# Cosine attention and hard-swish feed-forward on one core: tensors relaid, instruction order fixed by hand, feed-forward matmuls spread over the attention, one activation table

## The chip, the cores and the metric

One core of one Trainium2 chip runs the whole program; the other seven are idle. The metric is device time in microseconds (us) of that core. Each kernel was run several times, beside runs of the kernel before on the same chip; a figure such as 771.4 us is the median of the runs. Profiles are of one execution, so the span on a profile page differs a little from the median.

## The reference, cut to what matters

```python
# q, k, v: (8 batches, 12 heads, 448 tokens, 64) float32; tau = 0.1
q_n = q / (norm(q) + 1e-6);  k_n = k / (norm(k) + 1e-6)      # over the last axis
scores = q_n @ k_n.T / tau
attn = exp(scores - max);  attn = attn / (sum(attn) + 1e-9)
x = (attn @ v), as (3584 tokens, 768)
h = x @ w_in                        # 768 x 2048
g = h * clip(h + 3, 0, 6) / 6       # hard swish
out = g @ w_out                     # 2048 x 768, float32
```

Cosine scores lie between -10 and 10, so neither kernel takes the maximum off before the exponential. Both compute in bf16 with fp32 sums.

## The kernel before

Two heads of a batch are one *pair*; there are 48. Tokens are cut in four chunks of 112. Results of TensorE (PE) go to PSUM, the memory that ScalarE and VectorE then read them from. A *bank* here is a piece of PSUM of 128 x 512 fp32, and a *tile* is a named buffer of one or two banks. A *unit* is the group of matmuls that fills one bank with a part of a feed-forward layer; to *evacuate* it is to read it out, which frees the bank. The parts that the argument touches:

```python
    def attention_pre(b, hp, slot):           # loads and norms
        nc.gpsimd.dma_start(out=qk_t[:CH, 0:8, :], in_=q_r[:, b, hA : hA + 2, :, :])   # casts to bf16
        ...  # k, v likewise; squares and reduce_sum on VectorE
        nc.scalar.activation(out=ln_t[:CH, :], in_=n2_t[:CH, :], func=AF.Ln)
        nc.scalar.activation(out=r_t[:CH, :], in_=ln_t[:CH, :], func=AF.Exp, scale=-0.5)
    ...
    def attention_core(b, hp, emit_backfill):
        for c in range(NCH):
            ...  # sc_ps = scores of 112 keys x 448 queries, both heads
            nc.scalar.activation(out=attn_t[:CH, :, :], in_=sc_ps[:CH, :, :S], func=AF.Exp, scale=inv_tau)
            nc.tensor.matmul(pv_ps[:, 0, :S], v_t[:CH, c, :], attn_t[:CH, 0, :], ...)   # [v, ones] stationary
            ...
            if c == 1:
                emit_backfill(1)
        nc.scalar.activation(out=lnd_t[D:128, :, :], in_=pv_ps[D:128, :, :S], func=AF.Ln)
        nc.scalar.activation(out=recd_t[D:128, :, :], in_=lnd_t[D:128, :, :], func=AF.Exp, scale=-1.0)
        ...  # xT = values * recd_t, on VectorE
    ...
    def moe_mm1_unit(blk, fc, half):          # one unit of the first layer
        ps1 = psum.tile([128, S], FP32, name="mm1_ps", tag="moe", bufs=4)
        ...  # six matmuls; relu on ScalarE or clip on VectorE; product on VectorE
```

The line numbers in the profile: L189 and L196 are scores, L203 the exponential, L209 and L216 values, L228 and L229 the logarithm and the exponential that together make the reciprocal of the softmax sums, L128 and L129 the same for the norms, L263 and L310 the two feed-forward layers. The order on each engine is left to the framework's scheduler.

## Time and profile before

| | kernel before |
|---|---|
| median time | 771.4 us |
| PE, VectorE (DVE), ScalarE (ACT), GpSimd (POOL) busy | 72%, 52%, 71%, 26% |
| table loads on ScalarE | 180, 231.0 us |
| PE waits for an exponential (L203) | 155.1 us (score matmuls 96.4, value matmuls 58.7) |
| first first-layer matmul | 59 us |

A busy share is an average over the span, so it does not say what the bound is; the chain that ended last does, and the waits say who held whom. A group line of the profile reads: source line, engine, operation, output and inputs, shape, how often; then busy us and mean ns of one; then the idle time of the engine just before it and what ended that. A wait line reads: who waited for whom, us in total, how often, the longest. The lines of this kernel are in the prediction below.

### The profile page before, as it was taken

What the parts mean: (1) busy time and instruction counts of PE and PEld (TensorE: products, weight loads), DVE (VectorE), ACT (ScalarE), POOL (GpSimd) and SP (SyncE); (2) the same over time, 40 slices, a digit from 0 to 9 for tenths busy, and PEclk for the clock granted to TensorE, in tenths of its full rate; (3) what the DMA queues carried; (4) which work ended last, traced back from release to release, by engine and by line L of the source; (5) the groups of instructions that cost most, each with busy time, mean ns of one, the idle gap of its engine ahead of it and who ended that gap; (6) DMA issues with size and microseconds to landing.
All of it is one profiled execution on the core that took longest, in us unless ns stands there. A gap on an engine that the chain in (4) does not pass through costs nothing.

```text
span 770.8 us, 7902 instructions
## 1 busy us (share of the span) xinstructions
PE 557.4 (72%) x2816; PEld 291.3 (38%) x2816; DVE 399.1 (52%) x682; ACT 549.6 (71%) x628; POOL 198.2 (26%) x316
## 2 busy tenths in 40 slices
PE   2546648656776767676866676789687799984998
PEld 1223214322333334343433333445344355542464
DVE  5645646666565625333755666334566633452722
ACT  3799897888798897788788889655678752466200
POOL 9435543323323222212223132222122110000000
PEclk9999668877789989999879999989899999998899
DMA  9969975535516334414435225332233012100011
GB/s 72 101 81 124 107 95 36 37 22 38 37 12 43 40 42 52 44 37 44 31 23 33 18 20 45 49 56 63 27 21 22 7 38 76 44 0 1 1 73 71
DMA packets 142600, 34.34 MB, mean 45 GB/s; under 512 B 132576, under 2 KB 141792, under 8 KB 142560
## 3 DMA queue, kind: packets, MB, share of 16 engines
q0 software_dynamic: 134496, 22.82, 38.5%
q1 hardware_dynamic: 8064, 11.01, 3.9%
q8 instruction: 22, 0.36, 0.2%
q14 instruction: 18, 0.15, 0.1%
HBM read 45.61 MB, written 11.01 MB: 73 GB/s over the span
## 4 chain that ended last, share of the span: by engine, by line
ACT 55%; PE 35%; issue 5%; DVE 4%; DMA 1%; POOL 1%; ACTq 0%; DVEq 0%; POOLq 0%
ACT attn_t L203 16%; PE mm_ps L310 12%; PE mm_ps L263 9%; ACT L203 7%; ACT L228 6%; ACT L128 6%; ACT L129 5%; ACT lnd_t L228 5%; PE sc_ps L189 4%; ACT recd_t L229 4%; PE pv_ps L209 4%; PE sc_ps L196 3%; PE pv_ps L216 3%; ACT hs_r L272 2%; ACT L229 2%
## 5 line engine op out<-in xcount | busy, mean ns | idle before, releaser
L203 ACT ACTIVATE attn_t<-sc_ps 112x896 bf16<-112x896 f32 x192 | 175.6, 915 | 140.2 <-PE sc_ps L196 120.2
L263 PE MATMUL mm_ps<-xT,w_in_sb 128*128 128x448 bf16 x768 | 192.6, 388 | 18.6 <-DVE xT L235 7.5
L310 PE MATMUL mm_ps<-w_out_sb,gT 128*128 128x384 bf16 x896 | 167.1, 336 | 4.0 <-DVE o_t L318 4.0
L189 PE MATMUL sc_ps<-qT_sb,bd_ka 128*112 128x448 bf16 x192 | 78.6, 410 | 104.6 <-ACT attn_t L203 96.4
L235 DVE TENSOR_TENSOR xT<-pv_ps,recd_t 64x448 bf16<-64x448 f32 x96 | 59.2, 617 | 149.6 <-ACT recd_t L229 145.6
L209 PE MATMUL pv_ps<-attn_t,v_t 112*128 112x448 bf16 x192 | 78.3, 408 | 61.0 <-ACT attn_t L203 58.7
L263 PEld LDWEIGHTS <-w_in_sb 128*128 128x128 bf16 x768 | 81.0, 106 | 97.3 <-issue 46.0
L310 PEld LDWEIGHTS <-gT 128*128 128x128 bf16 x896 | 89.5, 100 | 67.5 <-issue 11.2
L163 POOL MEMSET bd_ka<- 64x448 bf16 x48 | 22.4, 466 | 269.5 <-PE sc_ps L189 232.3
L196 PE MATMUL sc_ps<-qT_sb,bd_kb 128*112 128x448 bf16 x192 | 79.5, 414 | 0.0
L216 PE MATMUL pv_ps<-attn_t,v_t 112*128 112x448 bf16 x192 | 78.4, 408 | 0.0
L318 DVE TENSOR_SCALAR o_t<-mm_ps 128x384 f32<-128x384 f32 x56 | 30.7, 556 | 85.3 <-PE mm_ps L310 85.0
L196 PEld LDWEIGHTS <-bd_kb 128*112 128x112 bf16 x192 | 28.3, 148 | 122.3 <-issue 116.4
L120 POOL DMA_DIRECT2D qk_t<-in_q_dram x48 | 39.5, 823 | 112.8 <-DVE kn_t L136 112.3
L279 DVE SCALAR_TENSOR_TENSOR gT<-hs_r,mm_ps 128x448 bf16<-128x448 bf16 x64 | 39.6, 619 | 44.0 <-ACT hs_r L272 43.4
L228 ACT ACT_TABLE_LOAD x47 | 60.3, 1283 | 0.8
L127 DVE TENSOR_REDUCE n_t<-sq_t 112x16 bf16<-112x1024 bf16 x48 | 57.9, 1215 | 0.8
L216 PEld LDWEIGHTS <-v_t 112*128 112x128 bf16 x192 | 20.6, 107 | 96.9 <-issue 91.7
L272 ACT ACTIVATE hs_r<-mm_ps,three_bias 128x448 bf16<-128x448 f32 x64 | 40.0, 630 | 23.5 <-PE mm_ps L263 20.7
L128 ACT ACT_TABLE_LOAD x43 | 55.2, 1283 | 1.5 <-PEq L390 0.7
L203 ACT ACT_TABLE_LOAD x42 | 53.9, 1283 | 1.5 <-PE sc_ps L196 0.8
L122 POOL DMA_DIRECT2D v_t<-in_v_dram x48 | 39.4, 820 | 53.3 <-PE pv_ps L216 44.6
(33 smaller groups left out, 623.2 us busy)
## 6 DMA issues: line engine op xcount, KB each, us to landing
out_dram<-o_t SPq DMA_DIRECT2D x56, 192.0 KB, 1.9
qk_t<-in_q_dram POOLq DMA_DIRECT2D x48, 112.0 KB, 3.3
qk_t<-in_k_dram POOLq DMA_DIRECT2D x48, 112.0 KB, 3.7
v_t<-in_v_dram POOLq DMA_DIRECT2D x48, 112.0 KB, 3.3
w_in_sb<-in_moe_w_in_dram POOLq DMA_DIRECT2D x6, 512.0 KB, 7.4
w_out_sb<-in_moe_w_out_dram POOLq DMA_DIRECT2D x16, 192.0 KB, 6.3
```

What stands on the lines that cost most here:

```text
L127: nc.vector.reduce_sum(n2_t[:CH, :], sq_t[:CH, :, :], axis=AX.X)
L128: nc.scalar.activation(out=ln_t[:CH, :], in_=n2_t[:CH, :], func=AF.Ln)
L189: nc.tensor.matmul(sc_ps[:CH, 0, :S], bd_ka[:, c * CH : (c + 1) * CH], qT_sb[:, :], start=True, stop=True,)
L196: nc.tensor.matmul(sc_ps[:CH, 1, :S], bd_kb[:, c * CH : (c + 1) * CH], qT_sb[:, :], start=True, stop=True,)
L203: nc.scalar.activation(out=attn_t[:CH, :, :], in_=sc_ps[:CH, :, :S], func=AF.Exp, scale=inv_tau,)
L209: nc.tensor.matmul(pv_ps[:, 0, :S], v_t[:CH, c, :], attn_t[:CH, 0, :], start=(c == 0), stop=(c == NCH - 1),)
L216: nc.tensor.matmul(pv_ps[:, 1, :S], v_t[:CH, 4 + c, :], attn_t[:CH, 1, :], start=(c == 0), stop=(c == NCH - 1),)
L228: nc.scalar.activation(out=lnd_t[D:128, :, :], in_=pv_ps[D:128, :, :S], func=AF.Ln)
L235: nc.vector.tensor_tensor(out=xT[p0 : p0 + 64, h // 2, b * S : (b + 1) * S], in0=pv_ps[0:D, hh, :S], in1=recd_t[D:128, hh, :], op=ALU.mult,)
L263: nc.tensor.matmul(ps1[:, :], w_in_sb[:, cc, fc * 128 : (fc + 1) * 128], xT[:, cc, tcol : tcol + S], start=(cc == 0), stop=(cc == CC - 1),)
L272: nc.scalar.activation(out=r_hs[:, :], in_=ps1[:, :], func=AF.Relu, bias=three_bias[:, :], scale=1.0,)
L310: nc.tensor.matmul(ps2[:, :], gT[:, fc, tci * 128 : (tci + 1) * 128], w_out_sb[:, fc, m * MH : (m + 1) * MH], start=(fc == 0), stop=(fc == ...
```

## The change

The intent is to make TensorE (PE) the bound and to keep it busy. The kernel is rewritten nearly whole, so only the core of the diff is shown:

```diff
+    ctx.enter_context(tc.manual_schedule())                       # fixed order
+    nc.scalar.preload_act_table_set("natural_log_exp_and_others") # one table
 ...
-    CH = 112
-    NCH = S // CH
+    SM = 384              # three chunks of 128 tokens of each head,
+    SR = S - SM           # and one of the last 64 tokens of both heads
 ...
+    X = [psum.tile([128, 2, 512], FP32, name=f"X{i}", tag=f"X{i}") for i in range(3)]
+    Y = psum.tile([128, 512], FP32, name="Y", tag="Y")
+    Z = psum.tile([128, 1024], BF16, name="Z", tag="Z")
+    moe_banks = [X[2][:, 0, :], X[2][:, 1, :], Y[:, :]]
 ...
-        nc.gpsimd.dma_start(out=qk_t[:CH, 0:8, :], in_=q_r[:, b, hA : hA + 2, :, :])
+            nc.sync.dma_start(out=raw[:, :, 4 * n : 4 * n + 3, :], in_=main(t))   # fp32, runs of 768 bytes
 ...
-            nc.tensor.matmul(pv_ps[:, 0, :S], v_t[:CH, c, :], attn_t[:CH, 0, :], ...)
+                nc.tensor.matmul(o, at[:, n, q_cols(i // HP, j)], mv, ...)        # exp stationary, [v, 1] moving
 ...
-        nc.scalar.activation(out=lnd_t[D:128, :, :], in_=pv_ps[D:128, :, :S], func=AF.Ln)
-        nc.scalar.activation(out=recd_t[D:128, :, :], in_=lnd_t[D:128, :, :], func=AF.Exp, scale=-1.0)
+        nc.vector.reciprocal(out=rc[:, :, :], in_=pv4[:, :, :, D])
 ...
+    for f in range(4):                                            # all weights, after pair 2's squares
+        nc.gpsimd.dma_start(out=w_in_sb[:, :, f * FG : (f + 1) * FG], ...)
+    for f in range(4):
+        nc.gpsimd.dma_start(out=w_out_sb[:, 4 * f : 4 * f + 4, :], ...)
 ...
+    for i in range(NP):                                           # 48 pairs, four slots each
+        for s in range(4):
+            ...                                                   # ns: this slot's share of feed-forward work
+            scores(i, s, next_sc(i))                              # two matmuls, one exp
+            if s == 0:
+                ...
+                fill(0.6 * ns); values(i - 1, 3); finish_values(i - 1); fill(0.4 * ns)
+            ...
+            else:
+                fill(ns)
+                values(i, 2)
```

(The slot loop is put on fewer lines here.) Squares, normalisation and the cast of v go to GpSimd (for the first two pairs, squares and normalisation stay on VectorE). Relus of the first layer are all on ScalarE and products all on VectorE. In the lines of the profile after, L163 are scores, L167 the exponential, L195 values, L238 and L267 the two layers, L248 the relu and L251 the product that read a first-layer unit out of PSUM.

## The prediction

> **What bounds the kernel now.** I read the page first (busy shares and the chain that ended last), then the groups of instructions by line, then the waits, then one pair of heads in order of time. The page, engine shares and the chain by engine:
>
> ```profile
> PE 557.4 (72%) x2816; PEld 291.3 (38%) x2816; DVE 399.1 (52%) x682; ACT 549.6 (71%) x628; POOL 198.2 (26%) x316
> ...
> ACT 55%; PE 35%; issue 5%; DVE 4%; DMA 1%; POOL 1%; ACTq 0%; DVEq 0%; POOLq 0%
> ```
>
> No engine is full, and over half of the chain lies on ScalarE (ACT). The groups by line say what ScalarE does with it:
>
> ```profile
> L203 ACT ACTIVATE attn_t<-sc_ps 112x896 bf16<-112x896 f32 x192 | 175.6, 915 | 140.2 <-PE sc_ps L196 120.2
> ...
> L228 ACT ACT_TABLE_LOAD x47 | 60.3, 1283 | 0.8
> ...
> L128 ACT ACT_TABLE_LOAD x43 | 55.2, 1283 | 1.5 <-PEq L390 0.7
> L203 ACT ACT_TABLE_LOAD x42 | 53.9, 1283 | 1.5 <-PE sc_ps L196 0.8
> ```
>
> With the loads of L129 (43.6 us) and L229 (18.0 us) in the longer list these are 180 loads, 231.0 us: 30% of the span, and 42% of ScalarE's busy time. The waits show the ping-pong that results: the score matmuls, the exponential and DVE's last multiply wait for one another.
>
> ```profile
> DVE xT L235 <- ACT recd_t L229: 145.6, 46, 11.9
> ACT attn_t L203 <- PE sc_ps L196: 120.2, 76, 11.4
> ...
> PE sc_ps L189 <- ACT attn_t L203: 96.4, 58, 6.6
> ```
>
> And the end of one pair, in order of time (start, length):
>
> ```profile
> 486.43 1.28 ACT L228 ACT_TABLE_LOAD   x1
> ...
> 487.73 0.91 ACT L228 ACTIVATE lnd_t<-pv_ps 64x896 f32<-64x896 f32 x1
> ...
> 488.66 1.28 ACT L229 ACT_TABLE_LOAD   x1
> ...
> 489.95 0.95 ACT L229 ACTIVATE recd_t<-lnd_t 64x896 bf16<-64x896 f32 x1
> ...
> 490.93 1.25 DVE L235 TENSOR_TENSOR xT<-pv_ps,recd_t 64x448 bf16<-64x448 f32 x2 [5.84 <-ACT recd_t L229]
> ```
>
> The reader is to see 4.4 us of ScalarE for one reciprocal of softmax sums, more than half of it loads, while PE has only feed-forward work to fill with. Before 59 us there is none, and PE is busy 50.4 of the first 100 us, there mostly with starts 0.37 us apart instead of 0.19.
>
> **What the Trainium skill says.** (1) "ScalarE: Activation LUTs", What ACT_TABLE_LOAD costs: about 1283 ns a load, plus a drain of about 1380 ns; its section on table sets says that one set has both exp and ln. The trace agrees on 1283; no drain shows, the next activation starts some 20 ns after the load. (2) "TensorE: Matmul & The Clock Gate", Back-to-back issue gap: N/2.4 + 2.5 ns, so 189 ns for 448 columns and 162 for 384. Agrees: six L310 matmuls take 1.14 us, that is five gaps of 0.16 and one whole 0.34. For short matmuls with a weight load each the page gives about 81 ns at N=128; the trace differs, since four 112-column transposes start 50 ns apart. (3) "GPSIMD Engine Reference", Elementwise, side by side: 4497 ns for a tensor_tensor over 2048 fp32, some 2.2 ns an element; no run here shows it. (4) "DMA: Bandwidth & Descriptors", Queues, rings and completion order: an engine takes turns between queues, packet by packet. The trace can't show turns; in its first 115 us the DMA row stands near full.
>
> **The change part by part.**
>
> *ScalarE.* One table load is left: minus 230 us. The reciprocal leaves ScalarE (minus 43.8 + 45.4). Remaining: exponentials 144 x 0.915 + 48 of half size (0.915 - 448/1.2 ns = 0.54) = 158; relus 128 x 0.63 = 81 (twice as many as now); norms 96 x 0.213 = 20; half the output copies 28 x about 0.51 = 14. Sum 273 us against 549.6. ScalarE ceases to be the bound.
>
> *DVE.* Per pair: reduction 896/1024 of 1.215 = 1.08; four copies out of the transposes about 1.25; reciprocal and 512-element multiply 0.1 + 0.69; copy back 0.39; two small ones 0.13: 3.65 x 48 = 175. Feed-forward 128 x 0.62 = 79, output copies 28 x 0.56 = 16. Sum 270: under now's 399. GpSimd: square and normalise 896 fp32 elements at 2.2 ns each, plus a 512-element cast of about 0.8: an estimate of 4.8 us a pair from page (3), so 225 us; hidden later, near the pace in the first phase.
>
> *PE.* The built program has 3872 matmuls: 768 x 189 = 145; 896 x 162.5 = 146; scores 336 x 189 = 63.5; transposes 528 x 56 = 29.6; values with exp(scores) stationary and 65 moving columns 1344 at a chosen 45 ns (estimate, below the 50 ns of the 112-column transposes) = 60.5. Sum **444 us**. So PE is now the floor, if nothing makes it wait.
>
> *The start.* The order puts no feed-forward matmul ahead of pair 7, and before that stand 22.8 of the 444 us. Until then pairs run at the latency of the chain score, exp, values, transpose and copies, or at GpSimd's 4.8 us, or PE's 6.5 us at half clock: about 5.5 x 7 after some 16 us of loads and normalisation before the first exp (which stands behind two more pairs' norms in ScalarE's order) = 55. All weights are now asked for at about 10 us, together with the loads. Weights are 12.6 MB of HBM reads; between 57.8 and 77 us, with full queues, the kernel before landed 124 GB/s in bf16, so read about twice that in fp32: some 50 us of all DMA, and each pair's 0.69 MB takes turns with it. I add 10: first feed-forward matmul at **65 us**.
>
> *The new wait.* The order of waits in the built program matters most. Three PSUM banks take turns, but two of them are halves of one tile X2, and I traced each matmul's semaphore value back to its producer: a unit that enters the second half of X2 waits for the DVE read of the unit **just before it**, in the first half, though the data differ. So each third unit starts only after its predecessor is evacuated. The price from the trace: from the start of the last matmul to the activation 0.44 (499.17 to 499.61), relu 0.63, step 0.04, DVE 0.62, step 0.04 = 1.77, less the gap of 0.19: 1.58 us (1.57 in the sums). There are 42 such entries after first-layer units, and attention matmuls between cover 0.08 us of it on average: 62.6 us. 19 after second-layer units, 0.85 us each with 0.32 cover: 13.2. Entries two units behind add 4.7. Sum **80.5 us** of bare PE stall. ScalarE and DVE are each some 45% busy (273 and 270 of 603) with other things, of 0.4 to 1.9 us at a time and in strict order (DVE's norms wait for two activations in the middle): 0.4 us more on each of 61 entries and 0.2 on 43 others = **33**.
>
> *Sum:* 65 + (444 - 22.8) + 80.5 + 33 + 3 for the last store = **603 us**. Gain: 168 us.
>
> **The rivals.** (A) *Dense PE.* If the bank waits cost little, 65 + 421 + 3 + some 10 = about 500. For it: the author spreads work by the nanosecond, and the stretch 600 to 680 us of the kernel before already runs PE 76.3 of 80 us busy. Against: the waits stand in the program, and nothing but 0.08 us stands between. (B) *The exponential becomes the bound again.* In the steady part all scores use one double bank X0, so scores s+1 wait for exp s: 0.44 + 0.915 + 0.04 = 1.4 us, against 1.55 us of fill per slot. Relus ahead of it in ScalarE's order can push it over: 164 slots x 0.3 = 50 us more, so about 650. Partly the same time as the bank stalls, so I don't add it. (C) *A slow start.* If loads are really starved until the weights are in, pair 7 starts at 85 or 90: about 625. The DMA row near full in the kernel before speaks for it; 768-byte runs where there were 256-byte ones (132,576 of 142,600 packets are now under 512 B) speak against. (D) *Short matmuls with their weight loads cost 80 ns*, as page (2) has it: 1344 x 35 = 47 more. Against: the 50 ns transposes.
>
> **Range and chances.** The floor that I can hardly doubt is 45 + 415 + 70 + 3 = 533; B, C and D each add 20 to 50 and seldom all. I take 545 to 660. To come within 2% of now, 755, three of the rivals would have to be full size at once: faster 0.97.
>
> **What would show it.** One ACT_TABLE_LOAD and ScalarE near 270 us. PE busy or pipelined most of the span, the chain over half PE. In the waits: PE on the first-layer line waiting for DVE's gT line, some 40 to 60 times at 1.5 to 2.2 us, sum 80 to 110 us; the same for the second layer, 10 to 25. First first-layer matmul at 55 to 80 us. Value matmuls some 45 ns apart. GpSimd's two-input operations near 2 us. I am wrong if those bank waits are few or short (A), if PE's longest sum is on exp (B), or if the first 100 us hold the time (C).

## The result, and the profile after

The changed kernel takes 627.7 us (625.8 to 629.7) against 771.4 us. The ratio is 0.814 (95% interval 0.811 to 0.817). A ratio is the mean time of one kernel's runs over that of the other's runs of the same rounds, so it isn't quite the ratio of the medians. Executions over 1.5% slower than the fastest of the same kernel are left out of the means. All outputs are right.

The page of the kernel after, engine shares and the chain by engine:

```profile
PE 468.8 (75%) x3872; PEld 282.0 (45%) x3872; DVE 284.5 (46%) x667; ACT 260.4 (42%) x445; POOL 187.9 (30%) x154
...
PE 54%; DVE 18%; ACT 12%; DMA 7%; issue 5%; SPq 3%; POOL 0%; DVEq 0%; ACTq 0%; POOLq 0%
```

ScalarE went from 549.6 to 260.4 us and from 55% to 12% of the chain. PE now leads it, but a quarter of the span PE does nothing. The groups by line that matter, and after them one of PE's waits in front of the scores, to which later runs are compared:

```profile
L238 PE MATMUL X<-xT,w_in_sb 128*128 128x448 bf16 x510 | 122.9, 356 | 78.3 <-DVE gT L251 77.7 <-DVE o L281 0.5
L267 PE MATMUL X<-w_out_sb,gT 128*128 128x384 bf16 x608 | 118.5, 328 | 20.9 <-ACT o L279 9.4 <-DVE gT L251 7.6 <-DVE o L281 3.9
...
L238 PE MATMUL Y<-xT,w_in_sb 128*128 128x448 bf16 x258 | 62.0, 359 | 0.0
...
L54 ACT ACT_TABLE_LOAD x1 | 1.3, 1283 | 0.7 <-PEq L431 0.7
```

```profile
PE X L163 <- ACT at L167: 15.5, 17, 6.4
```

In both feed-forward layers all of the waiting stands in front of matmuls into X (here the tile X2, of two banks). Matmuls of these layers into Y, a tile of one bank, never waited. One such wait, in order of time (start, length; in square brackets the idle time before):

```profile
300.76 1.11 PE L238 MATMUL X<-xT,w_in_sb 128*128 128x448 bf16 x5
...
301.91 0.63 ACT L248 ACTIVATE u<-X,half_bias 128x448 bf16<-128x448 f32 x1
302.57 0.62 DVE L251 SCALAR_TENSOR_TENSOR gT<-u,X 128x448 bf16<-128x448 bf16 x1 [1.13 <-ACT u L248]
...
303.25 0.92 PE L238 MATMUL X<-xT,w_in_sb 128*128 128x448 bf16 x4 [1.26 <-DVE gT L251]
```

A unit ends in one half of X2, its relu and its product run one after the other, and only then does PE write the other half. The beginning, from the chain in order of time (start, length, what):

```profile
18.34 7.94 DMA raw<-in_q_dram
26.30 9.76 DMA raw<-in_q_dram
36.08 13.22 DMA raw<-in_q_dram
49.31 12.51 DMA raw<-in_q_dram
```

From 18 to 62 us the chain is almost nothing but loads. The first feed-forward matmul starts at 79 us, later than in the kernel before. The span cut there (columns as in the busy shares; the count of instructions in brackets; then PE's clock, DMA's share, GB/s):

```profile
0.00:79.00 79.00, 36.77 (x323) 23.20 (x324) 40.93 (x111) 26.88 (x49) 40.36 (x40) 0.83 0.89 185
79.00:624.00 545.00, 432.04 (x3551) 258.79 (x3548) 243.61 (x556) 233.53 (x396) 147.50 (x115) 0.99 0.24 67
```

So two questions are open: what do the bank waits cost, and what holds up the beginning? And a third: which part of the change made the gain?

### The profile page after: what moved, and what is told of

It reads as the page before. It is cut to its first block, busy times and chain, and to the rows that moved or that the text cites. A ratio compares the mean times of both kernels' runs of the same rounds, so it can differ in the third digit from the quotient of the medians.

```text
span 624.0 us, 9913 instructions
## 1 busy us (share of the span) xinstructions
PE 468.8 (75%) x3872; PEld 282.0 (45%) x3872; DVE 284.5 (46%) x667; ACT 260.4 (42%) x445; POOL 187.9 (30%) x154
## 4 chain that ended last, share of the span: by engine, by line
PE 54%; DVE 18%; ACT 12%; DMA 7%; issue 5%; SPq 3%; POOL 0%; DVEq 0%; ACTq 0%; POOLq 0%
PE X L267 15%; PE X L238 13%; DVE gT L251 7%; PE X L163 7%; PE Y L267 7%; DMA raw<-in_q_dram 7%; ACT u L248 6%; PE X L195 6%; DVE n L110 5%; PE Y L238 4%; ACT at L167 3%; DVE xT L222 2%; PE Z L221 1%; PE Z L133 1%; DVE o L281 1%
## 5 line engine op out<-in xcount | busy, mean ns | idle before, releaser
L167 ACT ACTIVATE at<-X 128x896 bf16<-128x896 f32 x192 | 156.6, 820 | 152.4 <-PE X L163 152.2
L238 PE MATMUL X<-xT,w_in_sb 128*128 128x448 bf16 x510 | 122.9, 356 | 78.3 <-DVE gT L251 77.7
L120 POOL TENSOR_TENSOR nrm<-raw,r 128x896 bf16<-128x896 f32 x46 | 77.8, 1691 | 225.6 <-DVE r L114 225.6
L238 PEld LDWEIGHTS <-w_in_sb 128*128 128x128 bf16 x768 | 72.9, 99 | 138.6 <-issue 86.3
L267 PE MATMUL X<-w_out_sb,gT 128*128 128x384 bf16 x608 | 118.5, 328 | 20.9 <-ACT o L279 9.4
L267 PEld LDWEIGHTS <-gT 128*128 128x128 bf16 x896 | 85.2, 98 | 78.6 <-issue 26.8
L163 PE MATMUL X<-qT,kz 128*128 128x448 bf16 x336 | 102.0, 376 | 17.8 <-ACT at L167 15.5
L101 POOL TENSOR_TENSOR sq<-raw 128x896 f32<-128x896 f32 x46 | 77.4, 1684 | 107.1 <-DMA raw<-in_q_dram 61.1
L251 DVE SCALAR_TENSOR_TENSOR gT<-u,X 128x448 bf16<-128x448 bf16 x85 | 52.7, 620 | 97.5 <-ACT u L248 96.5
L195 PE MATMUL X<-vx,at 128*128 128x65 bf16 (+1 forms) x1344 | 75.0, 204 | 19.7 <-ACT at L167 19.7
L195 PEld LDWEIGHTS <-at 128*128 128x128 bf16 x1344 | 66.9, 102 | 48.3 <-ACT at L167 22.1
L248 ACT ACTIVATE u<-X,half_bias 128x448 bf16<-128x448 f32 x85 | 53.6, 631 | 38.8 <-PE X L238 36.9
L238 PE MATMUL Y<-xT,w_in_sb 128*128 128x448 bf16 x258 | 62.0, 359 | 0.0
L110 DVE TENSOR_REDUCE n<-sq 128x14 f32<-128x896 f32 x48 | 51.7, 1077 | 18.9 <-POOL sq L101 18.8
L267 PE MATMUL Y<-w_out_sb,gT 128*128 128x384 bf16 x288 | 56.1, 326 | 0.0
L163 PEld LDWEIGHTS <-kz 128*128 128x128 bf16 x336 | 31.0, 102 | 35.6 <-issue 19.6
L251 DVE SCALAR_TENSOR_TENSOR gT<-u,Y 128x448 bf16<-128x448 bf16 x43 | 26.6, 619 | 16.2 <-ACT u L248 15.6
```

The lines of the kernel that those rows point to most:

```text
L101: eng.tensor_tensor(out=sq[:, :, :], in0=a, in1=a, op=ALU.mult)
L110: nc.vector.tensor_reduce(out=n2[:, :], in_=sq[:, :, :], axis=AX.X, op=ALU.add)
L120: eng.tensor_tensor(out=nrm[:, :, :, :].rearrange("p s h d -> p h s d"), in0=raw_of[i][:, :, :, :], in1=r_of[i][:, :].rearrange("p (h s) - ...
L163: nc.tensor.matmul(sc[:, n, 0:S], k_block(i, name), qT_of[i][:, :], start=True, stop=True)
L167: nc.scalar.activation(out=at[:, 0:m, :], in_=sc[:, 0:m, 0:S], func=AF.Exp, scale=inv_tau)
L195: nc.tensor.matmul(o, at[:, n, q_cols(i // HP, j)], mv, start=(name == "A0" and j % 2 == 0), stop=last, skip_group_check=True,)
```

## The experiments

Theory: (1) units wait for each other because two of the three banks belong to one tile (the *false wait*: the data differ), and this costs about 110 us; (2) the beginning is long because all weights are moved beside the first loads; (3) the table loads were most of the old bound. Each has a rival in the expectations.

### e1_rotation: another order of the banks

```diff
-        return moe_banks[bank_n[0] % 3]
+        return moe_banks[(0, 2, 1, 2)[bank_n[0] % 4]]
```

> Only the order in which feed-forward units take the three banks is changed: first half of X2, Y, second half of X2, Y. No unit then waits for the one just before it; 124 wait for the one two before. Theory (the shared tile makes the stalls): first-layer PE waits on gT fall from 77.7 us to 25 to 45, second-layer ones from 20.9 to under 8; time 628 -> 565 to 590. Rival (ScalarE and VectorE in their fixed order are the pace, the bank only shows it): the wait moves to scores on exp or to other banks, time above 610.

Measured: 547.1 us, ratio to before 0.709 (0.707 to 0.711): 80.6 us less than the changed kernel, and 18 us under the range that I had written, since the false wait costs more than the 98.6 us of listed waits by which I had reckoned (see e2). The waits that stay:

```profile
PE Y L238 <- DVE gT L251: 19.2, 25, 2.6
...
PE X L238 <- DVE gT L251: 6.4, 8, 1.9
PE Y L267 <- DVE gT L251: 6.1, 6, 1.2
```

31.7 us in 39 waits. (The built program has 137 entries two units behind; my count of 124 was short.) With a whole unit between, most of an evacuation is covered, not all. No instruction was changed in this run, and none was taken off ScalarE or VectorE, so these engines were not the pace.

### e2_split: two tiles in place of one

```diff
-    X = [psum.tile([128, 2, 512], FP32, name=f"X{i}", tag=f"X{i}") for i in range(3)]
+    X = [psum.tile([128, 2, 512], FP32, name=f"X{i}", tag=f"X{i}") for i in range(2)]
+    XP = [psum.tile([128, 512], FP32, name=f"XP{i}", tag=f"XP{i}") for i in range(2)]
-    moe_banks = [X[2][:, 0, :], X[2][:, 1, :], Y[:, :]]
+    moe_banks = [XP[0][:, :], XP[1][:, :], Y[:, :]]
 ...
-        return X[0] if sc_n[0] % 2 else X[2]
+        return X[0] if sc_n[0] % 2 else XP      # where it is XP, the exp is cut in two, one for each tile
```

> X2 is made of two tiles of one bank each, so that a unit waits only for the third one before it; the few paired exps of the first phase are cut in two. Theory: PE waits of both layers on their evacuation fall from 98.6 us to under 20; time 628 -> 530 to 555. Rival (fixed order of ScalarE and VectorE is the pace): above 600, with PE waiting for exp instead.

Measured: 514.9 us (514.5 to 515.0), ratio 0.668 (0.666 to 0.669), 15 us under the range written. Both layers into the split tiles, then the span, cut at 79 us again:

```profile
L246 PE MATMUL XP<-xT,w_in_sb 128*128 128x448 bf16 x510 | 116.5, 352 | 0.0
L275 PE MATMUL XP<-w_out_sb,gT 128*128 128x384 bf16 x608 | 115.4, 326 | 0.0
```

```profile
0.00:79.00 79.00, 36.51 (x322) 23.08 (x323) 41.40 (x111) 26.82 (x55) 40.20 (x40) 0.83 0.89 185
79.00:513.00 434.00, 416.17 (x3551) 256.49 (x3549) 241.53 (x556) 230.68 (x396) 147.68 (x115) 1.00 0.29 84
```

The beginning is the same to within 0.3 us of PE work. The rest, with the same 3551 matmuls, takes 434 us instead of 545: **111 us were the false wait**. No matmul of either layer waits any longer. PE is busy 96% of that stretch. The listed waits of the changed kernel were only 98.6 us (77.7 + 20.9). PE's busy time in the stretch fell too, by 15.9 us, and its waits for exponentials rose by 4.4 (11.0 against 6.6): 98.6 + 15.9 - 4.4 = 110. The starts of the matmuls say where the 15.9 us come from: a first-layer matmul is shown 0.35 us long, but the next one starts 0.19 us after it when nothing waits, so one in front of a wait is shown with its whole length (an estimate from the starts: some 10 us of the difference). The other 6 to 7 us are matmuls in short stretches in which half the clock was granted (0.99 on average in this part of the span, against 1.00 in e2); these went together with the waits, and no run tells the two apart. The theory stands, the rival falls.

### e3_weights_late: weights one by one

```diff
-    for f in range(4):
-        nc.gpsimd.dma_start(out=w_in_sb[:, :, f * FG : (f + 1) * FG], ...)   # and four of w_out
 ...
                     vcast(i + 2, nc.gpsimd)
+                if i >= 1 and i < 9:
+                    weights(i - 1)              # one of the eight transfers
```

> The eight weight transfers are issued one per pair from pair 1 on, not all at 16 us. Theory (weights take turns with the q, k, v loads and starve them): the gaps of 3 to 13 us between loads from 24 to 62 us go, first feed-forward matmul at 50 to 60 us instead of 79, time 628 -> 600 to 612. Rival (the loads are slow by their own issue, 0.6 us each and at most eight under way): first feed-forward matmul stays above 72 us, time above 620.

Measured: 611.4 us, ratio 0.792 (0.788 to 0.795); 16.3 us less than the changed kernel. One line of the first layer's matmuls (shortest, median and longest duration in ns, then the starts of the first and the last), then the span cut there:

```profile
L238 PE MATMUL X<-xT,w_in_sb x510: 349/352/581, 59.7 to 575.4; 128*128 128x448 bf16 x170
```

```profile
0.00:59.50 59.50, 29.25 (x322) 18.43 (x323) 40.72 (x111) 26.55 (x49) 35.77 (x36) 1.00 0.85 184
59.50:605.00 545.50, 432.35 (x3551) 258.51 (x3549) 242.64 (x556) 233.53 (x396) 152.18 (x118) 0.99 0.27 73
```

The beginning shrinks from 79 to 59.5 us, the rest is unchanged (545.5 against 545). Loads hold 12 us of the chain in it, where they held 43 before. So it was the weights beside the loads, and the two causes lie in different stretches. The granted clock of the beginning differs as well (1.00 against 0.83); with both mendings (e5) it is 0.89, and the beginning is still 62 us long. The profiled run is 6 us faster than the median, the changed kernel's 4 us; by the medians the gain is 16.3 us, by the two profiles 19.0.

### e4_two_banks: the suspected wait doubled

```diff
-        return moe_banks[bank_n[0] % 3]
+        return moe_banks[bank_n[0] % 2]
```

> The suspected wait doubled: only the two halves of X2 take turns, so nearly every unit waits for the one just before it (120 instead of 40 first-layer entries one behind, 48 instead of 17 second-layer ones). Theory: 80 more entries at 1.6 to 2.0 us and 31 more at 0.85 to 1.1, less some 15 us for the entries two behind: 628 -> 750 to 800. Rival (the stall hides other waits that would be there anyway): under 700.

Measured: 810.2 and 822.1 us in two runs (two more, of 824.6 and 830.2, were slow), ratio 1.058 (1.049 to 1.068): slower than the kernel before, and above the range written.

```profile
PE X L238 <- DVE gT L251: 186.1, 120, 3.0
PE X L267 <- ACT o L279: 23.7, 28, 2.3
...
PE X L267 <- DVE o L281: 12.5, 20, 1.0
PE X L267 <- DVE gT L251: 11.8, 8, 2.1
```

234.1 us of such waits instead of 98.6, in exactly the 120 first-layer places that the built program names. The rise in waits is 135.5 us, that in the profiled span 184.5 (808.5 - 624.0). The other 49 are PE's own: it is busy 516.7 us instead of 468.8 for the same work, partly by the whole lengths shown in front of waits and partly because its mean granted clock was 0.916 instead of 0.967 (an estimate from the matmuls' starts: some 21 and 24 us). I had left the clock out.

### e5_split_late: both mendings

> The two mendings together: X2 as two tiles, and one weight transfer per pair. Theory (the two causes lie in different stretches and add up): 514.9 less the 16.3 us that late weights gained on the changed kernel, so 494 to 502; first feed-forward matmul near 60 us, PE busy 95% after it. Rival (a denser kernel needs the weights sooner, so PE waits for them): above 508.

The edit is that of e2 and e3 together. Measured: 495.9 us (495.4 to 498.9), ratio 0.644 (0.641 to 0.646). Busy shares, and the stretches before and after 62 us (the first feed-forward matmul starts at 62.8):

```profile
PE 450.3 (91%) x3872; PEld 278.1 (56%) x3872; DVE 285.3 (57%) x667; ACT 257.4 (52%) x451; POOL 187.9 (38%) x154
```

```profile
0.00:62.00 62.00, 33.61 (x321) 21.47 (x322) 41.00 (x111) 26.58 (x55) 35.77 (x36) 0.89 0.86 185
62.00:497.00 435.00, 416.67 (x3555) 256.62 (x3552) 244.27 (x556) 230.79 (x397) 152.14 (x118) 1.00 0.33 91
```

The gains add up: 112.9 and 16.3 us alone (against 627.7), 131.8 together. This is the fastest version: 21% less than the changed kernel, 36% less than the kernel before. What stays is the beginning, in which PE has 34 us of work in 62.

### e6_no_preload and e9_split_late_no_preload: the table line undone

```diff
-    nc.scalar.preload_act_table_set("natural_log_exp_and_others")
```

> The changed kernel without the line that loads the one table: 96 loads instead of 1, two in each pair around the norms, 122 us of ScalarE. Theory (ScalarE is 42% busy and not the bound, but the loads delay relus and exps that stand behind them in order, and VectorE waits for the norms in the middle): 640 to 690. Rivals: all hidden, 628 to 635; or all exposed, above 740.

Measured: 705.9 us, ratio 0.915 (0.913 to 0.916), so 78 us more than the changed kernel, above the range written. 96 loads of 1283 ns are 123 us. PE's wait for products in front of the first layer rose from 77.7 to 95.9 us and its wait for exponentials in front of scores from 15.5 to 32.7:

```profile
PE X L237 <- DVE gT L250: 95.9, 58, 4.7
PE X L162 <- ACT at L166: 32.7, 32, 8.2
```

Not all of the 78 us are waits: PE is also busy 32.3 us longer for the same work (501.1 against 468.8), at a mean granted clock of 0.922 against 0.967. Whether the loads bring the lower clock is not shown, so e9, where the clock hardly moves (0.981 against 0.985), is the cleaner measure.

> The mended kernel (e5_split_late, 495.9 us) without the line that loads the one table: again 96 loads, 122 us of ScalarE. In the changed kernel the same step cost 78 us. Theory (there the loads delayed relus, whose banks PE waited for; with three free banks more of it is hidden): 520 to 560. Rival (ScalarE is 52% busy already and with the loads over 70%, so its order is the pace and less is hidden): above 575.

The same line taken from e5: 554.6 us, ratio 0.719 (0.717 to 0.721), 58.8 us more than e5. With free banks nearly all of the new waiting stands in front of the scores (e5, then this run):

```profile
PE X L164 <- ACT at L175: 18.3, 30, 6.5
```

```profile
PE X L163 <- ACT at L174: 65.1, 53, 8.0
```

So about half of the loads' time is exposed here (58.8 of 123 us), though ScalarE is busy only 69% of the span; in e6, its lower clock included, it is nearly two thirds. The loads stand in order in front of an exponential whose bank PE needs next.

### e7_before_preload: that line alone, in the kernel before

```diff
+    nc.scalar.preload_act_table_set("natural_log_exp_and_others")
     half_bias = const.tile([128, 1], FP32, name="half_bias", tag="half_bias")
```

> The kernel before with that one line alone: 1 load instead of 180, so 230 us less of ScalarE, which holds 26% of the chain (some 200 us) as table loads. Theory (the loads were most of the bound): 771 -> 590 to 660, so that this one line gains as much as the whole change. Rival (the chain of score, exp, value and reciprocal in turn stays the bound in the old arrangement): above 690.

Measured: **589.0 us** (583.8 to 590.0), ratio 0.762 (0.759 to 0.766).

```profile
PE 510.1 (87%) x2816; PEld 275.9 (47%) x2816; DVE 397.7 (68%) x682; ACT 320.5 (54%) x449; POOL 198.8 (34%) x316
```

```profile
PE sc_ps L190 <- ACT attn_t L204: 27.3, 45, 2.6
PE pv_ps L210 <- ACT attn_t L204: 14.6, 17, 1.9
```

PE's waits for exponentials fall from 155.1 to 41.9 us, and PE's busy time for the same work from 557.4 to 510.1, at a mean granted clock of 0.950 against 0.898; whether fewer waits brought the higher clock, no run tells. This one line takes off 182.7 us, more than the whole change (143.7) and a little more than the range written. The other parts of the change, as they were put together, *lost* 38.7 us on top of it. Without the line in either kernel they gain 65.5 us (771.4 to 705.9, e6; the new kernel then has 96 loads, the old 180): the parts overlap, and what one is worth depends on which others are there. With the false wait and the weights mended the others gain 93 us on top of the line (589.0 to 495.9).

### e8_split_bunched: the spreading undone

```diff
-                fill(0.6 * ns)
+                pair_ns = 4 * ns
 ...                                             # fill(0.4 * ns), fill(0.8 * ns) and so on: taken out
-                fill(ns)
+                fill(pair_ns)
                 values(i, 2)
```

> Compared with e2_split, 514.9 us: the feed-forward matmuls of a pair are no longer spread over its four slots but stand together in the last one. Theory (spreading hides exp behind PE work: without it three of four score groups wait 0.8 to 1.2 us for the one X0 bank, and transposes wait for VectorE's copies): 3 us a pair on 41 pairs, 514.9 -> 600 to 650. Rival (the wait is covered by the long stretch of fill that follows): under 540.

Measured: 604.3 us, ratio 0.783 (0.782 to 0.784), 89.4 us more than e2_split, inside the range. The wait lines of e2_split and then of this run:

```profile
PE X L164 <- ACT at L175: 20.1, 32, 6.9
```

```profile
PE X L164 <- ACT at L175: 94.1, 125, 6.3
```

The same exponentials of the same length, now with nothing beside them: 125 waits instead of 32. The spreading is worth 89 us, once the banks are free.

## Why the prediction was right or wrong, point by point

The predicted time was 603 us in a range of 545 to 660; 627.7 was measured. By the steps of the prediction:

- **"Minus 230 us" of table loads; ScalarE at 273 us, no longer the bound: right.** One load, 260.4 us, 12% of the chain. (VectorE came to 284.5 us against 270; its first term should read 1.06, not 1.08, which changes nothing.) What the prediction did not see is how much of the whole gain this one line could make alone (e7).
- **The new wait, 80.5 + 33 = 113.5 us: right in mechanism and in size.** 57 waits, 77.7 us, in front of the first layer and 22, 20.9 us, of the second (10, 5 and 7 by who released them) were found, and e2 puts the cost at 111 us. The order of the units in the trace tells the entries apart, since every third unit enters the second half of X2. One behind, 41 first-layer units waited 68.0 us and 19 second-layer units 18.9; the prediction's terms for these come to 62.6 + 13.2 + 24.4 = 100. Two behind, 20 units waited 12.3 us, against 4.7 + 8.6 = 13.3. The listed waits fall short of the stalls by the lengths shown in front of them (e2). The forecast of the list itself was a little high: 57 waits have a mean of 1.36 us, not 1.5 to 2.2, and their sum is just under the 80 to 110. One sum of it is wrong as written: 19 entries of 0.85 us less 0.32 make 10.1, not 13.2.
- **The start, 65 us: wrong by 14.** It was 79 us. The failed term is "I add 10" for the weights' turns with the loads: they cost 19.5 us in the profile (e3, 79 to 59.5). Rival (C) was closer, with 85 or 90 us. Without weights the start estimate was 55 us, and e3 has 59.5: the other 4.5 of the 14. The prediction's own range for that matmul, 55 to 80 us, just held it.
- **PE's work after the start, 444 - 22.8 = 421 us, and 3 us for the last store: 424 predicted, 434 found in e2.** PE is busy 416 of these 434 us, 13.3 us are waits for an exponential, a copy or a normalisation, for which the sum had no term, and some 4 us at the end have no matmul. One term in it was mis-sized: value matmuls were put at 45 ns. Eight of 65 columns take 0.24 us up to the start of the next group, so 30 ns each (kernel after, in order of time):

```profile
300.14 0.41 PE L195 MATMUL X<-vx,at 128*128 128x65 bf16 x8
...
300.38 0.54 PE L163 MATMUL X<-qT,kz 128*128 128x448 bf16 x2
```

  One in seven moves 130 columns and takes longer, and so does the step to the next group: over all 1152 after the start in e2 the mean from one start to the next is 39 ns, which makes 7 us less than predicted. That this miss and the waits partly cancel is luck.
- **Rival (A), dense PE at 500 us:** false for the kernel as it stands, and nearly what the mended one does (e5, 495.9).
- **Rival (B), scores wait for exp:** the line that would show it has 15.5 us in 17 waits, 6.6 of them after the start. False here; it is true when the fill is bunched (e8).
- **Rival (D), short matmuls with weight loads at 80 ns:** false, 30 ns.
- **GpSimd "near 2 us" for two-input operations:** 1.69 us, so 4.0 us a pair with the cast; not on the path.

The sum came out 24.7 us low. By the profile, the start is 14 of it and the rest of the span 7 (545 against 421 + 3 + 113.5 = 538: without the false wait 10 more, as above, and the false wait 2.5 less); 3.7 lie between this profile and the median.

## What to carry to other kernels

When buffers take turns, look in the built program at which release each user waits for: two banks cut from one tile were treated as one, and that cost 111 us of 628 with nothing in the source that looks like a wait. Before a rewrite, try its cheapest line alone: here one preloaded table gave more than all parts together, and the loss that the other parts made beside it could not be seen in the whole. Move what is needed late after what is needed now, even when both fit on average: DMA was busy 89% of the first 79 us, and 24% of the rest.

## What the Trainium skill lacked or had wrong

- "TensorE: Matmul & The Clock Gate", Back-to-back issue gap, gives about 81 ns for 128 columns and 131 ns for 512 in a stream of matmuls with a weight load each, and keeps its formula N/2.4 + 2.5 ns for an isolated matmul. Here, in such streams at full clock, the median from start to start was 56 ns for 128 columns (transposes), 162 for 384 and 189 for 448, and 30 ns for 65 columns: the formula's values, not the stream's.
- "ScalarE: Activation LUTs", What ACT_TABLE_LOAD costs: 1283 ns is what all loads here took. The drain of about 1380 ns beside it does not show: in e6 an activation that began at 302.52 us took 0.21, the load after it began at 302.75, and the next activation at 304.04.
- No page has it: that the framework orders accesses to two separate banks of one PSUM tile as if they were one; 111 us here.
- No page has a figure for how long a load holds the queue of SyncE when it is issued there: mostly 0.48 to 0.62 us each here (0.59 with two runs in each of 128 partitions), so the seven of a pair held it some 4.4 us in the first 18 us.
